# A three-stage kernel in which the gated block's weight items are begun one item ahead and rounds of a gate normalization move to later places

## The chip, the core and the metric

The kernel runs on one core of a Trainium2 chip, in one launch. The time is device microseconds of the whole execution, as the median of several runs; a run with a profile gives a trace beside its time. Every time below comes from the times, the page or the trace of the kernel before.

## What is computed

The reference chains three blocks, each of which feeds the next. The first, attention with a bias from a small network, is not touched and is left out here.

```python
def _moe_ref(x, w1, w2, w3, w_out) -> np.ndarray:          # x (1152, 512), w1..w3 (512, 768)
    h = np.maximum(np.maximum(x @ w1, x @ w2), x @ w3)
    return (h @ w_out).astype(np.float32)

def _moe2_ref(x, w_gate, w1, w2) -> np.ndarray:            # N, D, E, F = 1152, 512, 8, 1024
    ...
    logits = x @ w_gate
    logits = logits - logits.max()
    P = np.exp(logits)
    for _ in range(8):
        P /= P.sum(1, keepdims=True) + 1e-09
        P /= P.sum(0, keepdims=True) + 1e-09
        P *= N / E
    out = np.zeros((N, D), dtype=np.float32)
    for e in range(E):
        h = np.maximum(x @ w1[e], 0.0)
        ye = h @ w2[e]
        out += P[:, e:e + 1] * ye
    return out.astype(np.float32)
```

## The kernel before

Everything is issued by one Python function. It writes each engine's program in the order in which its steps are called, and each engine works through its own program in that order, so a step that waits holds up what stands behind it on its engine. A program of waits between engines is worked out from the tiles that they read and write. T is TensorE, V is VectorE (DVE), A is ScalarE (ACT), G is GpSimd (POOL); DMAs are issued by SyncE (SP). A tile's bufs says how many buffers its name has; a tile waits until the last reader of the buffer that it takes is done.

**Gated block** (second block, from about 211 to 368 us of the span, its output product included). Numbers are split into a high and a low part, and every product is three matmuls: high by high, low by high, high by low. Weights come as 64-bit words in 24 items, in the order of `w_items`: first the three matrices of slice f = 0, then for each of six slices f the three `w` items of the next slice and one `o` item (a part of w_out). One item goes through `prep_w64`: ScalarE takes the absolute value of the upper words into a tile ww (L113), VectorE makes four passes over it (L114, L115, L117, L119, of which the last two read the raw words wr as well), ScalarE copies the high part (L121, wh or woh), and GpSimd subtracts it to get the low part (L122, wl or wol). For an `o` item VectorE also takes a maximum (L111). When an item is through, the DMA of item i + 2 is issued, since there are two raw buffers wr; ww has two buffers as well.

The loop runs over six slices f and three groups g of 384 tokens. A group's matmuls are `m1_mm` (L657): two matrices into m01, 24 matmuls, and the third into p2, 12. Behind the first two ScalarE copies m01 to t1 (L886), VectorE takes the maximum (L888), then, after p2, a second one (L891), and ScalarE writes hh (L892); VectorE's low part and maximum of the group stand in the next one (L895, L799). In between `w_step(6)` and `w_step(4)` issue the next six and four steps of the weight items. Then w_out's product (L1069) gives 16 tiles in the order of `k`; ScalarE evicts them with a scale into acc (L1073), and the steps of `sched[k]` are issued behind tile k.

**Experts** (third block). The program goes up0, up1, up2, down0, up3, up4, down1, up5, up6, down2 and so on to the end: `up(n)` makes half an expert's hidden layer in seven products (L1218) out of 2x2 blocks of x and w1 and sums of them, into the banks x, y and z; ScalarE snaps a bank into s (L1226), VectorE joins a product to it (L1230), ScalarE writes the high part hh (L1234) and VectorE the low part hl (L1239). After each product `then(seg)` issues what `between` and `extra` hold for that place. `x_steps(s)` names the sums of x's blocks for token half s: t1, t2, tb, t4 on VectorE (L971), `h2` to `h6` their high parts (xth, L965, ScalarE) and `l2` to `l6` their low parts (xtl, L961). `m_top` and `m_spread` bring one maximum to all partitions and make the scalars cx, with which the first snapshot is scaled. `down(h)` makes nine output tiles t (L1298), evicted into acc by ScalarE for h = 0 (L1303) and by VectorE else (L1309 for h = 1, L1314); behind tile t it issues the weight work of the coming halves (`todo`: prep_f, L937 to L956, and prep_2, L1029 to L1031).

**The gates' normalization** is eight rounds, each `rows()` (L1147 to L1150) and then `cols(bank)`: one matmul with ones (L1154) and four VectorE instructions (L1155 to L1158), all on the tile P of 128x72. Before, they stand behind tiles of down0, in up3, up4 and down1. P is needed first by `pool_scale`, which multiplies acc by expert 0's gate on GpSimd (L68, nine times), and by `gains(2)` in up6.

## Time and profile before

| what | value |
|---|---|
| median of 3 runs | 1092.28 us (1091.94 to 1093.19) |
| the profiled execution's own time | 1092.72 us |
| its span in the trace | 1090.9 us |
| mean granted TensorE clock | 0.989 |
| TensorE busy | 1051.1 us, 96% of the span |
| VectorE busy | 799.6 us, 73% |
| ScalarE busy | 589.2 us, 54% |
| GpSimd busy | 408.9 us, 37% |

Busy time is the time in which at least one instruction of the engine runs; matmuls follow each other before the one before has ended, so that their durations overlap. A busy share of 96% is a mean over stages: where an engine stops is read from the list of its waits, each with what released it, and what the other engines do in such a stretch from the busy time by stretch and from the groups of instructions by line (busy time, mean duration of one, and the idle time just before them, with what ended it). A timeline gives single instructions with start and duration; "xN" behind a row joins N like ones.

### The profile page before, as it was taken

To read this page: it belongs to the slowest core of one execution; us is meant where nothing else is said; L and a number is where in the kernel's file an instruction comes from. 1 tells how busy PE (TensorE), PEld (TensorE's weight loads), DVE (VectorE), ACT (ScalarE), POOL (GpSimd) and SP (SyncE) were. 2 spreads that over 40 slices of the span, in tenths; PEclk is the share of its full clock that TensorE was granted. 3 is DMA by queue.
4 is the path that set the end of the run, shared out by engine and by line. 5 is a ranking of instruction groups with operands and counts; after the bars stand their busy time and mean duration, and the time that the engine had idled before them with its cause. 6 is when DMAs were issued, how large, how long until landed. Compare 5 with 4: busy or idle time off the path is not lost.

```text
span 1090.9 us, 18480 instructions
## 1 busy us (share of the span) xinstructions
PE 1051.1 (96%) x7163; PEld 736.3 (67%) x7163; DVE 799.6 (73%) x1549; ACT 589.2 (54%) x1003; POOL 408.9 (37%) x285
## 2 busy tenths in 40 slices
PE   7789999999999999999999999999999999999998
PEld 3269988999889765655756657566466575665753
DVE  8989999778776878867677566676776666767633
ACT  7989988434334666444544536445455364454530
POOL 6996998122222424053231312412223124132220
PEclk8989999999999999999999999999999999999999
DMA  5888664233324012120221211302212113020002
GB/s 190 273 242 263 225 192 119 65 108 113 94 58 155 21 42 73 29 63 21 63 63 40 63 35 50 82 20 64 56 46 64 35 50 82 20 44 6 1 1 87
DMA packets 40757, 90.48 MB, mean 83 GB/s; under 512 B 8095, under 2 KB 11102, under 8 KB 39774
## 3 DMA queue, kind: packets, MB, share of 16 engines
q1 hardware_dynamic: 40526, 89.01, 28.6%
q8 instruction: 56, 0.92, 0.4%
q10 hardware_dynamic: 144, 0.29, 0.1%
q14 instruction: 31, 0.25, 0.1%
HBM read 75.20 MB, written 13.30 MB: 81 GB/s over the span
## 4 chain that ended last, share of the span: by engine, by line
PE 65%; DVE 20%; ACT 5%; DMA 4%; issue 4%; POOL 2%; DVEq 0%; ACTq 0%; SPq 0%; POOLq 0%
PE d L1298 27%; PE x L1218 11%; PE y L1218 8%; PE z L1218 7%; PE sc L468 3%; PE o L1069 2%; PE pv L606 2%; PE m L657 2%; PE pt L554 2%; DMA all<-peaks 2%; DVE pk L799 1%; DVE ng L485 1%; DVE ww L114 1%; DVE ww L119 1%; DMA peaks<-pj 1%
## 5 line engine op out<-in xcount | busy, mean ns | idle before, releaser
L1298 PE MATMUL d<-w2h,hh 128*128 128x512 f16 x576 | 218.3, 379 | 1.8 <-DVE acc L1309 1.7
L1298 PE MATMUL d<-w2h,hl 128*128 128x512 f16 x576 | 218.3, 379 | 0.2 <-DVE hl L1239 0.2
L1298 PE MATMUL d<-w2l,hh 128*128 128x512 f16 x576 | 218.3, 379 | 0.0
L1218 PEld LDWEIGHTS <-w1h 128*128 128x128 f16 x1792 | 175.0, 98 | 53.3 <-issue 6.4
L1298 PEld LDWEIGHTS <-hh 128*128 128x128 f16 x1152 | 112.5, 98 | 134.8 <-issue 3.4
L950 POOL TENSOR_TENSOR w1l<-wf,w1h 128x768 f16<-128x768 f32 x32 | 55.7, 1742 | 304.4 <-ACT w1h L949 270.7
L1234 ACT ACTIVATE hh<-s 128x576 f16<-128x576 f32 x128 | 87.3, 683 | 129.0 <-DVE s L1230 101.5
L1239 DVE SCALAR_TENSOR_TENSOR hl<-s,hh 128x576 f16<-128x576 f32 x128 | 112.4, 879 | 48.1 <-ACT hh L1234 45.6
L1314 DVE SCALAR_TENSOR_TENSOR acc<-d,kh,acc 128x512 f32<-128x512 f32 x126 | 94.0, 746 | 67.1 <-PE d L1298 65.6
L1031 POOL TENSOR_TENSOR w2l<-w2r,w2h 128x512 f16<-128x512 f32 x64 | 77.4, 1221 | 120.0 <-ACT w2h L1030 120.0
L1218 PEld LDWEIGHTS <-w1l 128*128 128x128 f16 x896 | 87.7, 98 | 22.7 <-issue 0.6
L1298 PEld LDWEIGHTS <-hl 128*128 128x128 f16 x576 | 56.3, 98 | 68.6 <-DVE hl L1239 0.7
L956 POOL TENSOR_TENSOR w1l<-wf,w1h 128x1024 f16<-128x1024 f32 x32 | 69.2, 2164 | 75.9 <-ACT w1h L953 75.9
L937 ACT ACTIVATE wf<-wr,pw 128x1024 f32<-128x1024 f32 x32 | 36.5, 1141 | 96.9 <-DVE pm L772 96.9
L1226 ACT ACTIVATE s<-x,cx 128x576 f32<-128x576 f32 x96 | 70.4, 733 | 27.0 <-PE x L1218 26.4
L1230 DVE SCALAR_TENSOR_TENSOR s<-z,cx,s 128x576 f32<-128x576 f32 x64 | 52.3, 817 | 42.9 <-ACT s L1226 27.7
L1218 PE MATMUL x<-xth,w1h 128*128 128x288 f16 x384 | 78.5, 286 | 0.7 <-ACT s L1226 0.7
L1218 PE MATMUL x<-xtl,w1h 128*128 128x288 f16 x384 | 78.6, 286 | 0.4 <-DVE xtl L961 0.4
L1218 PE MATMUL x<-xth,w1l 128*128 128x288 f16 x384 | 78.4, 286 | 0.0
L953 ACT ACTIVATE w1h<-wf 128x1024 f16<-128x1024 f32 x32 | 33.6, 1049 | 82.9 <-DVE wf L946 82.9
L657 PE MATMUL m<-xh,wl 128*128 128x384 f32 x216 | 74.1, 343 | 2.9 <-POOL wl L122 2.9
L657 PE MATMUL m<-xh,wh 128*128 128x384 f32 x216 | 73.9, 342 | 2.5 <-DVE t L888 1.4
(227 smaller groups left out, 2371.7 us busy)
## 6 DMA issues: line engine op xcount, KB each, us to landing
wr<-in_moe_w SPq DMA_DIRECT2D x50, 512.0 KB, 3.6
w2r<-in_moe_w SPq DMA_DIRECT2D x64, 256.0 KB, 2.6
bias_f<-bo SPq DMA_DIRECT2D x36, 295.5 KB, 3.6
bias<-bias_f SPq DMA_DIRECT2D x32, 288.0 KB, 2.9
qk<-in_qk SPq DMA_DIRECT2D x7, 1152.0 KB, 7.2
wr<-in_moe_w_out SPq DMA_DIRECT2D x6, 512.0 KB, 3.5
vr<-in_v SPq DMA_DIRECT2D x8, 320.0 KB, 6.9
bias<-bias_f SPq DMA_DIRECT2D x16, 144.0 KB, 4.9
```

Of the source, the lines that this page charges most:

```text
L657: T.matmul(out=p[:, :TG], lhsT=ws[:, 128 * c:128 * c + 128], rhs=xs[:, c, TG * g:TG * g + TG], start=(c == 0 and n == 0), stop=(c == 3 and ...
L937: A.activation(out=t[:, 0:4], in_=w1r.pop(n), func=AF.Identity, scale=w_pow[n // 2, 1][:, 2:3])
L950: G.tensor_tensor(out=lo[:, 0:3], in0=t[:, 1:4], in1=hi[:, 0:3], op=ALU.subtract)
L956: G.tensor_tensor(out=lo[:, 3:7], in0=t[:, 4:8], in1=hi[:, 3:7], op=ALU.subtract)
L1031: G.tensor_tensor(out=lo, in0=r, in1=hi, op=ALU.subtract)
L1218: T.matmul(out=ps[bank][:, s, :SH], lhsT=ws[:, i, c, :], rhs=xs[:, j, c, s * SH:s * SH + SH], start=(start and k == 0), stop=(k == 5), **kw)
L1226: A.activation(out=t, in_=src, func=AF.Identity, scale=c)
L1230: V.scalar_tensor_tensor(out=out, in0=z, scalar=scale, in1=out, op0=ALU.mult, op1=ALU.add)
L1234: A.activation(out=o, in_=src, func=AF.Relu)
L1239: V.scalar_tensor_tensor(out=l, in0=src, scalar=0.0, in1=o, op0=ALU.max, op1=ALU.subtract)
L1298: T.matmul(out=pd, lhsT=hs[:, fh, 128 * t:128 * t + 128], rhs=ws, start=(k == 0), stop=(k == 11))
L1314: V.scalar_tensor_tensor(out=acc[:, t, :], in0=pd, scalar=kh[:, 1 + t:2 + t], in1=acc[:, t, :], op0=ALU.mult, op1=ALU.add)
```

## The change

It has three parts. (1) ScalarE's Abs of weight item i + 1 is issued among the VectorE passes of item i, between the second and the third (`start_w64`); from the start of the gated block on, every third raw item has a third buffer `wr3`, and the load that follows an item is that of item i + 3 in place of i + 2 (`load_item(5)` at the start makes up for the one that is missing). The tiles wh and wl of even slices come from one pool, of odd ones from another, three buffers each. (2) Of `x_steps(1)`, t1 is issued behind tile 14 in place of 15 and h2 is the first high part; tb, h4 and h5 go from behind tile 15 into up0. (3) The fifth row and fourth column round of down0, the pair in up3 and the column round of down1 leave their places; up5 gets two pairs, up6 one column round, up4's second pair stands one product earlier, and `pool_scale` goes from up5 to up6. The number of rounds stays eight.

```diff
@@ -88,8 +88,13 @@
 
-            def load_w64(src):
-                r = w1p.tile([128, 1024], I32, tag="wr", name="wr", bufs=2)
+            third = []
+
+            def load_w64(src, n):
+                if third and n % 3 == 2:
+                    r = third[0].tile([128, 1024], I32, tag="wr3", name="wr", bufs=1)
+                else:
+                    r = w1p.tile([128, 1024], I32, tag="wr", name="wr", bufs=2)
                 dma(r, src.bitcast(I32))
                 return r
 
@@ -98,22 +103,31 @@
-            def prep_w64(r, hi, lo, top_to=None):
-
-                words = r.rearrange("p (a n t) -> p a n t", a=4, t=2)
+            w_abs = {}
+
+            def start_w64(i):
+
+                if i in w_raw and i not in w_abs:
+                    top = w_raw[i].rearrange("p (a n t) -> p a n t", a=4, t=2)[:, :, :, 1]
+                    w_abs[i] = w1p.tile([128, 4, 132], I32, tag="ww", name="ww", bufs=2)
+                    A.activation(out=w_abs[i].bitcast(F32)[:, :, :128], in_=top.bitcast(F32), func=AF.Abs)
+
+            def prep_w64(i, hi, lo, top_to=None):
+
+                start_w64(i)
+                words = w_raw.pop(i).rearrange("p (a n t) -> p a n t", a=4, t=2)
                 top, low = words[:, :, :, 1], words[:, :, :, 0]
-
-                wp = w1p.tile([128, 4, 132], I32, tag="ww", name="ww", bufs=2)
+                wp = w_abs.pop(i)
                 w, f = wp[:, :, :128], wp.bitcast(F32)[:, :, :128]
                 hi, lo = (x.rearrange("p (a n) -> p a n", a=4) for x in (hi, lo))
 
                 peak = [] if top_to is None else [
                     lambda: V.tensor_reduce(out=top_to, in_=f, op=ALU.max, axis=AX.XY, apply_absolute_value=True)]
                 return [
-                    lambda: A.activation(out=f, in_=top.bitcast(F32), func=AF.Abs),
                     lambda: V.tensor_scalar(out=f, in0=f, scalar1=2.0 ** -15, scalar2=None, op0=ALU.max),
                     lambda: V.tensor_scalar(out=w, in0=w, scalar1=3, scalar2=0x3FFFFFFF,
                                             op0=ALU.logical_shift_left, op1=ALU.bitwise_and),
+                    lambda: start_w64(i + 1),
                     lambda: V.scalar_tensor_tensor(out=w, in0=top, scalar=-0x40000000, in1=w,
                                                    op0=ALU.bitwise_and, op1=ALU.bitwise_or),
                     lambda: V.scalar_tensor_tensor(out=w, in0=low, scalar=29, in1=w,
@@ -126,13 +140,13 @@
             w_at, w_steps = [0], []
-            w_pool = [w1p, 3]
+            w_pool = [w1p, None, None]
...
             def load_item(n):
                 if n < len(w_items):
                     kind, i = w_items[n]
                     w_raw[n] = load_w64(a[f"moe_w{i % 3 + 1}"][i // 3] if kind == "w"
-                                        else a["moe_w_out"][128 * i:128 * i + 128])
+                                        else a["moe_w_out"][128 * i:128 * i + 128], n)
@@ -143,10 +157,10 @@
                             return
                         kind, k = w_items[i]
                         if kind == "w":
-                            wt[k] = [w_pool[0].tile([128, 512], F32R, tag=t, name=t, bufs=w_pool[1]) for t in ("wh", "wl")]
-                        w_steps.extend(prep_w64(w_raw.pop(i), *(wt[k] if kind == "w" else wo[k]),
+                            wt[k] = [w_pool[k // 3 % 2].tile([128, 512], F32R, tag=t, name=t, bufs=3) for t in ("wh", "wl")]
+                        w_steps.extend(prep_w64(i, *(wt[k] if kind == "w" else wo[k]),
                                                 top_to=None if kind == "w" else mo[0][:, 18 + k:19 + k]))
-                        w_steps.append(lambda: load_item(i + 2))
+                        w_steps.append(lambda: load_item(i + (3 if third else 2)))
                         w_at[0] += 1
@@ -855,7 +869,9 @@
                 wol = [hp.tile([128, DM], F32R, name=f"wol{f}") for f in range(6)]
                 wo.update({f: (woh[f], wol[f]) for f in range(6)})
                 with pool("mp", bufs=2) as mp:
-                    w_pool[:] = mp, 6, None
+                    w_pool[1] = mp
+                    third.append(mp)
+                    load_item(5)
...
                          8: [b_all] + xs_("t1", "tb", "h2", "l2"), 9: xs_("h3", "h5", "t2") + pf1[1:3], 10: xs_("l3", "l5", "h4") + pf1[3:4],
                          11: xs_("l4", "t4") + pf1[4:6] + [pk(1, 2, 0)], 12: xs_("h6", "g6") + [bs1[0], pk(1, 2, 1), pk(1, 2, 2)],
                          13: [bs1[1], p2(0), pk(1, 2, 3), lambda: peak_join(*SC)], 14: [p2(1), lambda: peak_send(SC[0])],
-                         15: [lambda: last.update(x_steps(1))] + [end(n) for n in ("t1", "t2", "tb", "h3", "h4", "h5", "h2", "l2")]}
+                         15: [end(n) for n in ("t2", "h2", "l2", "h3")]}
+                sched[14] += [lambda: last.update(x_steps(1)), end("t1")]
@@ -1179,7 +1196,8 @@
-                between = {(0, 0): [m_top, end("l3")], (0, 1): [m_spread, end("l4"), end("l5")], (0, 2): [end("t4")],
+                between = {(0, 0): [m_top, end("h4"), end("l3")],
+                           (0, 1): [m_spread, end("l4"), end("tb"), end("h5"), end("l5")], (0, 2): [end("t4")],
                            (0, 3): [end("h6"), end("l6")], (0, 6): [p2(2)], (1, 5): [p2(3)],
@@ -1301,15 +1319,13 @@
                         if h == 0:
 
                             A.activation(out=acc[:, t, :], in_=pd, func=AF.Identity, scale=kh[:, 0:1])
-                            if t in (2, 4, 6, 8):
+                            if t in (2, 4, 6):
                                 cols(ps_u)
-                            if t in (0, 2, 4, 6, 8):
+                            if t in (0, 2, 4, 6):
                                 rows()
                         elif h == 1:
                             V.scalar_tensor_tensor(out=acc[:, t, :], in0=pd, scalar=kh[:, 0:1], in1=acc[:, t, :],
                                                    op0=ALU.mult, op1=ALU.add)
-                            if t == 2:
-                                cols(ps_u)
                         else:
                             V.scalar_tensor_tensor(out=acc[:, t, :], in0=pd, scalar=kh[:, 1 + t:2 + t], in1=acc[:, t, :],
                                                    op0=ALU.mult, op1=ALU.add)
@@ -1323,11 +1339,12 @@
                         extra = {}
                         if n == 1:
                             extra = {i: [f] for i, f in enumerate(prep_f(2))}
-                        for seg in {3: (4,), 4: (1, 5)}.get(n, ()):
+                        for seg in {4: (1, 4), 5: (1, 4)}.get(n, ()):
                             extra.setdefault(seg, []).extend((lambda: cols(ps_d), rows))
-                        if n == 5:
+                        if n == 6:
+                            extra[1] = [lambda: cols(ps_d)]
                             for t in range(NTT):
-                                extra.setdefault(t % 7, []).append(
+                                extra.setdefault(2 + t % 5, []).append(
                                     lambda t=t: pool_scale(acc[:, t, :], acc[:, t, :], P[:, t, 0:1]))
                         if n and (n % 2 == 0 or n == 4 * NE - 1):
                             extra.setdefault(3, []).append(lambda n=n: gains(n // 2 - (n % 2 == 0)))
```

On ScalarE in the gated block (slice f = 1), with the numbers of the tiles: before,

```order
L886 ACTIVATE t1_3862<-m01_3860 128x384
L121 ACTIVATE wh_3853<-ww_3855 128x512
L113 ACTIVATE ww_3899<-wr_3837 128x4x128
L892 ACTIVATE hh_3629<-t2_3863 128x384
L121 ACTIVATE wh_3897<-ww_3899 128x512
L886 ACTIVATE t1_3925<-m01_3923 128x384
```

and at the same place of the changed kernel:

```order
L902 ACTIVATE t1_3866<-m01_3864 128x384
L135 ACTIVATE wh_3857<-ww_3835 128x512
L113 ACTIVATE ww_3905<-wr_3841 128x4x128
L908 ACTIVATE hh_3631<-t2_3867 128x384
L135 ACTIVATE wh_3901<-ww_3861 128x512
L902 ACTIVATE t1_3929<-m01_3927 128x384
```

Before, the Abs that writes ww_3899 is followed by the high part of that same item; now the high part behind the Abs of ww_3905 is that of ww_3861, the item before it.

On ScalarE between the gated block's last tile and the first expert's second snapshot: before,

```order
L1073 ACTIVATE acc_3606<-o_5172,xs_3610 128x288
L965 ACTIVATE xth_4713<-t_5194 128x2x288
L965 ACTIVATE xth_4713<-t_5196 128x2x288
L965 ACTIVATE xth_4713<-t_5195 128x2x288
L965 ACTIVATE xth_4713<-acc_3606 128x2x288
L1226 ACTIVATE s1_5275<-x_5234,cx_5231 128x576
```

and now:

```order
L1090 ACTIVATE acc_3608<-o_5176,xs_3612 128x288
L981 ACTIVATE xth_4713<-acc_3608 128x2x288
L981 ACTIVATE xth_4713<-t_5172 128x2x288
L981 ACTIVATE xth_4713<-t_5174 128x2x288
L981 ACTIVATE xth_4713<-t_5173 128x2x288
L1244 ACTIVATE s1_5275<-x_5231,cx_5228 128x576
```

The copy out of acc (h2) goes from the last to the first place; the copy ahead of s1 is now h5, out of tb (t_5173), and tb stands on VectorE behind the scalars cx and l4:

```order
L1197 TENSOR_SCALAR cx<-cx,xs 128x1
L977 TENSOR_TENSOR xtl<-t,xth 128x2x288
L987 TENSOR_TENSOR t<-acc 128x576
L977 TENSOR_TENSOR xtl<-t,xth 128x2x288
L1248 SCALAR_TENSOR_TENSOR s_5275<-z,cx,s_5275 128x576
```

On VectorE at the start of up5, with the numbers of the tiles: before,

```order
L1230 SCALAR_TENSOR_TENSOR s_6397<-z,cx,s_6397 128x576
L1239 SCALAR_TENSOR_TENSOR hl<-s_6397,hh 128x576
L1230 SCALAR_TENSOR_TENSOR s_6447<-y,cx,s_6447 128x576
L1239 SCALAR_TENSOR_TENSOR hl<-s_6447,hh 128x576
L1270 TENSOR_TENSOR s_6431<-s_6477,s_6431 128x576
```

and now:

```order
L1248 SCALAR_TENSOR_TENSOR s_6371<-z,cx,s_6371 128x576
L1172 TENSOR_REDUCE col<-pc 128x8
L1173 TENSOR_SCALAR col<-col 128x8
L1174 RECIPROCAL col<-col 128x8
L1175 SCALAR_TENSOR_TENSOR P<-P,col 128x72
L1164 TENSOR_REDUCE row<-P 128x9
L1165 TENSOR_SCALAR row<-row 128x9
L1166 RECIPROCAL row<-row 128x9
L1167 TENSOR_TENSOR P<-P,row 128x72
L1257 SCALAR_TENSOR_TENSOR hl<-s_6371,hh 128x576
```

The eight instructions of a pair stand between the first join and its low part; the same eight stand again behind the second join (s_6426).

## Rows read from the trace of the kernel before

**Rows 1.** Waits of TensorE, whole span: waited for, us in total, times, longest us

```profile
PE m L657 <- POOL wl L122: 2.9, 4, 0.8
...
PE y L1218 <- ACT s L1226: 2.4, 2, 2.1
PE d L1298 <- DVE acc L1309: 1.7, 2, 0.9
...
PE m L657 <- DVE t L888: 1.4, 3, 0.6
...
PE m L657 <- ACT wh L121: 1.0, 1, 1.0
PE z L1218 <- DVE col L1155: 0.8, 1, 0.8
```

**Rows 2.** Timeline of TensorE, 229:231: start, duration us, instruction, idle before

```profile
229.05 0.34 PE L657 MATMUL m<-xh,wh 128*128 128x384 f32 x1
229.22 0.34 PE L657 MATMUL m<-xl,wh 128*128 128x384 f32 x1
230.21 0.44 PE L657 MATMUL m<-xh,wl 128*128 128x384 f32 x1 [0.65 <-POOL wl L122]
230.49 0.33 PE L657 MATMUL m<-xh,wh 128*128 128x384 f32 x1
```

**Rows 3.** Busy time by stretch: length, busy of five engines, PEclk, DMA share, GB/s

```profile
229.00:312.00 83.00, 77.64 (x437) 74.95 (x436) 65.44 (x117) 32.00 (x62) 21.85 (x17) 1.00 0.41 107
309.00:313.00 4.00, 2.16 (x11) 1.53 (x10) 2.76 (x6) 1.98 (x4) 1.28 (x1) 0.99 0.40 131
313.00:316.40 3.40, 3.40 (x13) 3.37 (x12) 3.30 (x6) 1.19 (x3) 0.47 (x1) 0.51 0.00 0
481.40:491.70 10.30, 10.30 (x86) 8.23 (x85) 5.78 (x7) 6.88 (x11) 10.30 (x10) 1.00 0.31 92
```

**Rows 4.** VectorE by line, 229:312: busy us, mean ns, idle before and releaser

```profile
L114 DVE TENSOR_SCALAR ww<-ww 128x512 f32<-128x512 f32 x17 | 12.8, 753 | 12.9 <-ACT ww L113 12.9
...
L115 DVE TENSOR_SCALAR ww<-ww 128x512 int32<-128x512 int32 x16 | 6.8, 424 | 0.4
...
L825 DVE TENSOR_REDUCE pj<-pk 128x1 f32<-128x2 f32 x1 | 0.2, 154 | 1.7 <-ACT acc L99 1.7
```

**Rows 5.** GpSimd by line, 229:312

```profile
L122 POOL TENSOR_TENSOR wl<-ww,wh 128x512 fp32r<-128x512 f32 x13 | 16.8, 1291 | 50.1 <-ACT wh L121 38.2 <-issue 11.8
```

**Rows 6.** ScalarE by line, 229:312

```profile
L113 ACT ACTIVATE ww<-wr 128x512 f32<-128x512 f32 x17 | 11.1, 654 | 2.4 <-DMA wr<-in_moe_w 2.4
```

**Rows 7.** Timeline of VectorE, 414.9:417.2 and 433:438

```profile
414.97 0.23 DVE L1155 TENSOR_REDUCE col<-pc 128x8 f32<-128x72 f32 x1 [0.24 <-PE pc L1154]
...
416.67 0.23 DVE L1150 TENSOR_TENSOR P<-P,row 128x72 f32<-128x72 f32 x1
...
433.02 0.22 DVE L1155 TENSOR_REDUCE col<-pc 128x8 f32<-128x72 f32 x1
...
435.62 1.72 DVE L1148 TENSOR_SCALAR row<-row 128x9 f32<-128x9 f32 x1
```

**Rows 8.** Timeline of GpSimd, 433:438

```profile
435.19 2.12 POOL L956 TENSOR_TENSOR w1l<-wf,w1h 128x1024 f16<-128x1024 f32 x1
```

**Rows 9.** Timeline of VectorE, 368.8:377

```profile
371.51 0.75 DVE L971 TENSOR_TENSOR t<-acc 128x576 f32<-128x576 f32 x1
...
373.85 0.21 DVE L1180 TENSOR_SCALAR cx<-cx,xs 128x1 f32<-128x1 f32 x1
```

**Rows 10.** Timeline of ScalarE, 368.8:377

```profile
373.84 0.74 ACT L1226 ACTIVATE s<-x,cx 128x576 f32<-128x576 f32 x1 [0.29 <-DVE cx L1178]
```

**Rows 11.** Timeline of TensorE, 372:379

```profile
375.57 0.28 PE L1218 MATMUL x<-xtl,w1h 128*128 128x288 f16 x1 [0.41 <-DVE xtl L961]
...
376.67 0.41 PE L1218 MATMUL y<-xth,w1h 128*128 128x288 f16 x2
```

**Rows 12.** GpSimd by line, 480:500

```profile
L68 POOL TENSOR_SCALAR acc<-acc,P 128x512 f32<-128x512 f32 x9 | 8.7, 986 | 0.0
```

## Prediction

> **What bounds the kernel now.** TensorE is busy for 96% of the span in the first part of the page, so only what makes it stop can be won. I read its waits first [rows 1]; there the reader is to see that three of them belong to the gated block's L657 (2.9, 1.4 and 1.0 us in 4, 3 and 1 times) and three to the start of the experts (2.4, 1.7 and 0.8 us), all of it work that this diff touches. Then I read TensorE's own starts at one such wait [rows 2]: matmuls follow each other by 0.17 us, the one that waited starts 0.65 us late, and the next comes 0.28 after it, 0.44 instead of 0.34 long; start to start the stall costs 230.49 - 229.22 - 2 x 0.17 = 0.93 us, that is its idle time and 0.28 more. Then the busy time in stretches [rows 3], to see which engine fills the stretch behind a wait, and the groups of VectorE, GpSimd and ScalarE in the gated block's 83 us [rows 4 to 6], to see what the busy time consists of and what each engine was waiting for.
>
> **Gated block, weight items one ahead.** In the stretch of 83.00 us TensorE is busy for 77.64, so idle for 5.4; the three waits give 2.9 + 1.4 + 1.0 = 5.3 [rows 1, 3]. With 0.28 us for each of the eight stalls that is 5.3 + 2.2 = 7.5 us. Right behind the stretch's end its granted clock is 0.51 for 3.40 us in which 13 matmuls run [rows 3], after 4.00 us in which TensorE was busy for only 2.16: at 0.17 us each they would take 2.2, so the low clock costs 1.2. That is 8.7 us to be had.
>
> What is late is VectorE. It is busy for 65.44 us of 83.00, and it idles 12.9 us ahead of the first pass over a weight item, L114, always for ScalarE's Abs of that item [rows 4]: 0.76 us for each of 17 items, near the 0.654 us that one Abs takes [rows 6]. The Abs stands on ScalarE just ahead of its own item's hi, and its VectorE passes follow at once. The change puts it a whole item earlier, so this idle time goes. The same Abs also waits 2.4 us for a weight load [rows 6]; with a third raw buffer a load is issued one item sooner, 83/17 = 4.9 us, and this wait goes too.
>
> A cover may go with it. L114 takes 753 ns where L115, the same form and size, takes 424 [rows 4]: L114 runs beside the previous item's lo on GpSimd (L122, 1291 ns [rows 5]). In the normalization the same is plain: a scalar step on 128x9 took 1.72 us and ended at 437.34, just behind a GpSimd operation that ended at 437.31, where a multiplication on 128x72 alone takes 0.23 [rows 7, 8]. So a VectorE step of this form started while GpSimd runs stands still until that ends. When L114 no longer waits for the Abs, it comes sooner after the previous hi and stands still for longer. Bounds: nothing more than now (0.33 an item) and a whole lo (1.29). Without blocking VectorE needs 65.4 - 17 x 0.33 = 59.8 us, and 1.7 for the size pass that it waits for [rows 4]; TensorE needs 83.0 - 7.5 = 75.5. The room is (75.5 - 61.5)/17 = 0.82 an item. I take 0.6, since L122 begins only behind the hi pass on ScalarE, in which VectorE can do a step of the group first. That leaves TensorE the bound, but not in every group: I leave 1.5 us of the 8.7 where single groups stay late. Term: **-7.2 us**, between -3.0 (blocking at 1.1) and -8.7.
>
> The Trainium skill, page "SBUF — State Buffer", section "Who interferes with whom", says that VectorE and GpSimd share one port pair under an exclusive lock, that a VectorE instruction with two SBUF inputs or in a two-port mode blocks fully beside a GpSimd one that reads SBUF, and that issue order decides which. The trace agrees in the blocked step's 1.72 us. Taken alone, that rule would let L114 be held for a whole lo each time, and the sum would be about -2.8; that is rival A.
>
> **Normalization, fewer rounds in down0, two more in up5.** One C and R pair (a column and a row round, eight VectorE instructions from L1155 to L1150) takes from 414.97 to 416.90 alone, 1.93 us; beside GpSimd its first six instructions take from 433.02 to 437.34, 4.3 us, and so the pair some 4.8 [rows 7]. The second one stands in up3, where z waits 0.8 us for col and y waits up to 2.1 us for a snapshot [rows 1]; the change takes it out. The 0.8 goes; of the snapshot's 2.4 I take the 2.1 that lies there: **-2.8** (bounds 0 if the weight items' ScalarE work alone keeps the snapshot late, -3.2 if both go). In down1 TensorE waits 1.7 us in two times for the eviction [rows 1], behind a column round that the change removes: four of eight instructions, half of 1.93 = 0.97 us. It clears the first (0.9) and half of the second: **-1.3** (bounds 0 and -1.7).
>
> The two pairs that are added to up5 stand ahead of hl, and z's bank is free only after the joins behind them. In the stretch of up5 VectorE is busy for 5.78 of 10.30 us [rows 3], so 4.5 us of slack. Two pairs cost 3.86, and one of them meets the lo of a weight part on GpSimd (2.12 us [rows 8]), a block of at most 1.72: 5.6, which is 1.1 over. With two column matmuls more on TensorE, 0.17 each: **+1.5** (bounds 0, if the block falls elsewhere, and 5.5, if both pairs take 4.8 like the one at 433: 9.7 - 4.5 + 0.3). The one column round that goes to up6 is half a pair, 0.97, below that slack. The nine scalings of acc on GpSimd [rows 12] go from up5 to up6: 8.7 us of a stretch of 10.30, covered by up6's own products, since the first use of acc is the first eviction behind them; without that cover each would cost 0.99. What they block on VectorE in up5 now, they block in up6. Sum of this part: **-2.6**, between -4.9 and +5.5.
>
> **Start of the first expert.** Before, ScalarE does all four xth copies (h2 to h5) and then the first product's snapshot s1; VectorE does t1, t2 and tb (L971) ahead of the scalars that s1 needs. Now t1 goes one tile of the gated block's output earlier, and tb, its copy h5 and l4 come between the scalars and s1, because h5 stands ahead of s1 on ScalarE. The scalars end at 374.06 now and s1 at 374.58 [rows 9, 10]. Two steps of L971 leave from ahead of the scalars, 0.75 us each [rows 9]: they end at 372.6, or up to 0.7 later if l3 has to wait for its copy. Behind them l4 and tb take 0.75 each, h5 and s1 0.74 each [rows 9, 10]: s1 ends at 375.6 to 376.3. The second product into s1's bank starts then. Now it starts earlier but stands before its fourth matmul until 375.57, for l4; the nine left take until 376.67 [rows 11], so twelve take 1.47, and the product behind starts at 377.1 to 377.8 in place of 376.67. Term: **+0.8**, between +0.4 and +1.2.
>
> **Sum.** -7.2 - 2.6 + 0.8 = -9.0 us. The profiled execution took 1092.72 us around its span of 1090.9; it becomes 1083.7. The median of the three runs shown is 0.44 lower, so 1083.3.
>
> **The rivals.**
> Forecast as above, 0.50. Low bound: all of the gated gain, the normalization's -4.9 and +0.4 at the first expert give -13.2; since all three together are unlikely I end the range a little above that, at 1079.5.
>
> Low clock again: if TensorE idles about as much at the first expert as in the 4.00 us before the low stretch (2.16 busy), the clock may fall there as it did at 313, for 1.2 us more; 1084.7. Against it: the idle time there comes in pieces. 0.17.
>
> Rival A, the lock takes the gated gain: each L114 is held 1.0 to 1.29 us, VectorE needs 61.5 + 17 x 1.29 = 83.4 us, all of the present stretch. For it: L114 comes nearer to the lo. Against: there is group work between. Only the 2.6 and the 0.8 and 1 us of clock remain, -2.8: about 1089.5. 0.12.
>
> Rival B, the added pairs run beside GpSimd in up5 as the one at 433 did, 4 us more: 1087.3. For it: GpSimd is busy for all of 10.30 us there [rows 3]. Against: most of that is the scaling, which leaves. 0.10.
>
> Rival C, slower: the Abs now stands ahead of hi and of the evictions of m on ScalarE, and needs one of two ww buffers, free only when GpSimd's lo of the item before the present one is done. If that lo is late, Abs waits and the evictions (t, hh) wait behind it, and VectorE behind those. It decides where the wait is over the 0.76 us an item that goes; at 1.0 us an item it costs 17 x 0.24 = 4.1, and the 7.2 are not won: with the other parts 1094.6. Against it: GpSimd idles 38.2 us for ScalarE's hi [rows 5], so the lo is seldom late. 0.06.
>
> Rival D: the gains at L657 turn up as waits at the block's last product, and nothing changes: 1092.3. 0.05.
>
> **How the numbers follow.** The forecast, the low clock, rival B and most of the ground toward A lie between 1079.5 and 1089.0, where I end the range: A's upper half, C and D, some 0.17, lie outside, and a little below. A measurement of this kernel can tell about 0.2%, 2.2 us, from no change. Faster by more than that: forecast, low clock, A and B, 0.89, less 0.01 for A's upper end, 0.88; the same, D and A's end, 0.06; slower, C, 0.06.
>
> **What would show it.** In the gated block: the waits of m for wl, t and wh below 1.5 us together, VectorE's idle time ahead of L114 (now two lines on in the code, same form) below 3 us and its mean up to 0.9 or 1.1; no stretch at a clock of 0.51 at the end. In up3: no wait of z for col, and that of y below 0.5. In down1: one wait for acc at most. In up5 to up6: a wait of about 1 us of z for s. At the first expert: s1 near 376, and y's snapshot behind it. Wrong would be: L114's mean at 1.2 or over (A), ScalarE idle ahead of Abs for POOL (C), C and R pairs of 4 us in up5 (B), or a gated block that is shorter by over 9 us.

## The result, and the profile after

The change takes 1082.68 us in the median of five runs (1080.69 to 1084.42), before 1092.28 (1091.94 to 1093.19): the ratio is 0.9911, with a 95% interval of 0.9899 to 0.9924, so 8.3 to 11 us faster. The forecast was 1083.3. The profiled execution of the change is the fastest of its five, 1080.69 us around a span of 1078.9, so that the two traces lie 12.0 us apart where the medians lie 9.6.

The waits of TensorE after, those that answer to [rows 1]:

```profile
PE x L1236 <- ACT s L1244: 3.4, 3, 2.3
...
PE y L1236 <- ACT s L1244: 0.9, 2, 0.6
PE z L1236 <- DVE s L1248: 0.6, 1, 0.6
...
PE d L1316 <- DVE acc L1327: 0.4, 1, 0.4
...
PE pc L1171 <- DVE P L1167: 0.3, 1, 0.3
```

No line for m is left in this list: the 5.3 us at L657 are gone, and so is z's wait for col. Of the waits behind attention one has grown by over 0.5 us: x for s, from 0.7 to 3.4, 2.3 of them in one piece. The busy time of the gated block's stretch, which answers to the first of [rows 3], and below it the groups of VectorE, ScalarE and GpSimd there, as in [rows 4 to 6]:

```profile
229.00:306.00 77.00, 77.00 (x445) 77.00 (x445) 73.03 (x126) 34.35 (x64) 22.67 (x17) 1.00 0.39 104
```
```profile
L131 DVE SCALAR_TENSOR_TENSOR ww<-wr,ww 128x512 int32<-128x512 int32 x18 | 15.9, 885 | 0.4
L133 DVE SCALAR_TENSOR_TENSOR ww<-wr,ww 128x512 int32<-128x512 int32 x18 | 12.4, 691 | 0.5
L127 DVE TENSOR_SCALAR ww<-ww 128x512 f32<-128x512 f32 x17 | 10.7, 631 | 0.2 <-ACT ww L113 0.2
L128 DVE TENSOR_SCALAR ww<-ww 128x512 int32<-128x512 int32 x17 | 9.4, 554 | 0.4
```
```profile
L113 ACT ACTIVATE ww<-wr 128x512 f32<-128x512 f32 x16 | 10.8, 674 | 17.3 <-POOL wl L136 11.1 <-DMA wr<-in_moe_w_out 3.2 <-POOL wol L136 2.1
```
```profile
L136 POOL TENSOR_TENSOR wl<-ww,wh 128x512 fp32r<-128x512 f32 x12 | 15.9, 1325 | 38.9 <-ACT wh L135 23.7 <-issue 11.0 <-PE m L671 4.3
```

TensorE is busy for all of 77.00 us, and VectorE for 73.03 of them, where it had been busy for 65.44 of 83.00. The reader is to see what became of VectorE's 12.9 us of idle time ahead of the first pass: 0.2 us are left. The waiting moved to ScalarE, whose Abs now waits 11.1 + 2.1 us for GpSimd's low parts and 3.2 for loads; it costs nothing here, since VectorE is an item behind. The stretching of the passes by GpSimd is there too, but spread: L127, L128 and L131 take 631, 554 and 885 ns, while L115 of before took 424 on the same size [rows 4] and L133 here, a pass of the form of L131, takes 691; so the three are 0.21 + 0.13 + 0.19 = 0.53 us an item longer.

Four starts of TensorE mark the stages of a trace: the first L657 (m) behind attention, the transposition pmw behind the gated block, pmx at the first expert, and the first product of down0. Before and after:

```profile
210.84 0.34 PE L657 MATMUL m<-xh,wh 128*128 128x384 f32 x1
...
330.43 0.27 PE L1000 MATMUL pmw<-ident,mho 128*2 128x128 f32 x1 [0.26 <-DVE mho L987]
...
369.70 0.27 PE L1170 MATMUL pmx<-ident,m 128*1 128x128 f32 x1 [0.36 <-DVE m L1083]
...
406.81 0.39 PE L1298 MATMUL d<-w2h,hh 128*128 128x512 f16 x1
```
```profile
210.10 0.34 PE L671 MATMUL m<-xh,wh 128*128 128x384 f32 x1
...
320.58 0.27 PE L1016 MATMUL pmw<-ident,mho 128*2 128x128 f32 x1 [0.26 <-DVE mho L1003]
...
359.86 0.27 PE L1187 MATMUL pmx<-ident,m 128*1 128x128 f32 x1 [0.36 <-ACT xth L981]
...
397.43 0.39 PE L1316 MATMUL d<-w2h,hh 128*128 128x512 f16 x1
```

These marks and those of the other traces, with the first product of down3 as the last one (545.94 before, 533.98 after), give this table (us; c1 and c2 are the change again, on two other chips; the experiments follow):

| trace | gated block, m to pmw | first expert, pmx to down0 | down0 to down3 |
|---|---|---|---|
| before | 119.59 | 37.11 | 139.13 |
| after; c1; c2 | 110.49; 110.49; 110.49 | 37.57; 38.13; 38.97 | 136.55; 137.79; 137.86 |
| e1, gated part alone | 110.49 | 37.08 | 141.17 |
| e2, first expert alone | 117.86 | 37.56 | 139.81 |
| e3, rounds alone | 120.23 | 37.11 | 137.71 |
| e4; e11, h5 late | 110.49; 110.94 | 36.11; 36.09 | 137.94; 137.54 |
| e5, third buffer without Abs ahead | 117.05 | 38.43 | 137.47 |
| e6, Abs ahead with two buffers | 120.80 | 40.20 | 137.58 |
| e8, pair in up6 | 110.49 | 38.14 | 136.96 |
| e9, low part on VectorE | 118.62 | 37.58 | 137.85 |
| e10, h5 late and pair in up6 | 110.93 | 36.11 | 137.10 |

Whole runs hold more than these stages. In the nine traces whose order of work is that of the change up to the first mark (after, c1, c2, e1, e4, e6, e8, e10, e11), that mark comes at 208.5 to 212.6 us. So a difference of 1 or 2 us between whole runs can't be given to a stage without the marks.

### The profile page after: what moved, and what is told of

Read it like the earlier page. It is cut to its first block, busy times and chain, and to the rows that moved or that the text cites. A ratio compares the mean times of both kernels' runs of the same rounds, so it can differ in the third digit from the quotient of the medians.

```text
span 1078.9 us, 18481 instructions
## 1 busy us (share of the span) xinstructions
PE 1044.3 (97%) x7163; PEld 734.6 (68%) x7163; DVE 800.3 (74%) x1549; ACT 590.3 (55%) x1003; POOL 410.0 (38%) x285
## 4 chain that ended last, share of the span: by engine, by line
PE 74%; DVE 14%; ACT 5%; DMA 3%; issue 2%; POOL 2%; DVEq 0%; ACTq 0%; POOLq 0%
PE d L1316 27%; PE x L1236 11%; PE m L671 11%; PE y L1236 8%; PE z L1236 7%; PE sc L482 3%; PE o L1086 2%; PE pv L620 2%; PE pt L568 2%; DMA all<-peaks 2%; DVE pk L813 2%; DVE ng L499 1%; DVE s L1248 1%; POOL s L356 1%; DVE hl L1257 1%
## 5 line engine op out<-in xcount | busy, mean ns | idle before, releaser
L671 PE MATMUL m<-xh,wh 128*128 128x384 f32 x216 | 72.9, 337 | 0.0
L671 PE MATMUL m<-xh,wl 128*128 128x384 f32 x216 | 72.8, 337 | 0.0
```

The costliest lines, as they stand in the source:

```text
L671: T.matmul(out=p[:, :TG], lhsT=ws[:, 128 * c:128 * c + 128], rhs=xs[:, c, TG * g:TG * g + TG], start=(c == 0 and n == 0), stop=(c == 3 and ...
```

## The experiments

The kernel before took 1096.3 us in the median on the three chips of the experiments (15 to 17 runs each, 1093.8 to 1099.7), 4 us more than on the first; so each kernel is compared with the runs of its own chip. Where an expectation names a whole time, it is worked out from the first chip's; the difference is what can be held against it.

**The three parts alone (e1, e2, e3).** Each is before with one part of the change's diff.

> Only the first part: Abs one item ahead, third raw buffer, the two pools of wh and wl. Theory (VectorE stood idle for the Abs, and the stalls of L657 with the low clock behind them were all of it): -7.2 to -8.7 us, so 1083.6 to 1085.1; no wait of m on wl, t or wh in the trace, idle time ahead of L114's counterpart below 1 us, and no stretch at clock 0.51 near 313. Rival 1 (the lock gives it back): mean of that step at 1.2 us or more and less than 3 us won. Rival 2 (the gain of the whole change comes from the rounds and the first expert): less than 2 us won.

> Only the second part: t1 one tile earlier, h2 first, tb, h4 and h5 between the scalars and the first snapshot. Theory (h5 ahead of s1 on ScalarE delays the second product into x more than the earlier scalars give): +0.4 to +0.8 us, 1092.7 to 1093.1, with one wait of x for s of about 2.3 us at the first expert and the 1.1 us wait of pmx gone. Rival (the edit helps, since the scalars come 1.2 us earlier): -0.5 to -1.2 us, 1091.1 to 1091.8, with less idle time of TensorE there.

> Only the third part: the rounds and the scaling of acc. Theory (each part as forecast: -2.8 in up3, -1.3 in down1, +1.5 in up5): -2.6 us, 1089.7, with the waits of y for s at 440 and of z for col at 433 gone, one wait for acc left in down1, and one of about 0.7 us of z for s behind up5. Rival 1 (the weight items' copies keep the snapshot late without the pair as well): y still waits 1 to 2 us for s in up3, -1 us at most, 1091.3. Rival 2 (up5's pairs run beside GpSimd): +1 us or more in all.

The gated part alone: 1088.20 us, ratio 0.9915 (0.9899 to 0.9932). Its gated block takes 110.49 us, to the hundredth what the change takes, with no wait at L657; the old block takes 117.86 and 120.23 on the same chip (e2, e3). It is the bulk of the change, and TensorE is the bound there. VectorE still idles 1.6 us ahead of the first pass, where less than 1 was expected. Both rivals fall.

The first expert alone: 1095.34 us, 0.9993 (0.9982 to 1.0004), not to be told from no change. The stage is 0.45 us longer (37.56 for 37.11), and its waits are those expected:

```profile
PE x L1220 <- ACT s L1228: 2.9, 2, 2.3
```

The rounds alone: 1092.38 us, 0.9961 (0.9947 to 0.9975). From down0 to down3 it takes 137.71 us, where the old places take 139.81 on the same chip (e2), and 141.17 with a stretch of low clock (e1); so 2.1 of the 4.0 us in the medians are shown in this stage. The waits of z for col and the long one of y went, but two of 0.5 and 0.6 us came in up3, so that rival 1 holds for a part:

```profile
PE x L1218 <- ACT s L1226: 1.2, 3, 0.5
...
PE y L1218 <- ACT s L1226: 0.9, 2, 0.6
...
PE z L1218 <- DVE s L1230: 0.7, 1, 0.7
```

In whole runs the three parts give -8.1, -1.0 and -4.0 us, together -13.1, more than the change's -10.7 and -9.6 (c1, c2). By stages they give what the change gives: 110.49, 37.56 and 137.71 beside 110.49, 38.13 and 38.97 (with the low clock), and 137.79 and 137.86. That the excess lies outside these stages is likely, but not shown: e3's trace reaches the first mark 2.6 us ahead of e2's, with the same order of work.

**The buffer without Abs ahead (e5), and Abs ahead without the buffer (e6), beside the change (c1).** Both keep the other two parts of the change.

```diff
 e5:
-                    lambda: start_w64(i + 1),
...
+                    lambda: A.activation(out=f, in_=top.bitcast(F32), func=AF.Abs), 
 e6:
-                    third.append(mp)
-                    load_item(5)
```

> The change itself, unaltered, on the chip and beside the runs of before that the next three share, so that they can be set against it. Theory: -8 to -11 us against before, with no wait of m on wl, t or wh; the chance part of it is TensorE's clock, which is 0.5 for 3.4 us at differing places.

> The change with the Abs of each weight item back at the item's own start; the third raw buffer and the earlier loads stay. Theory (VectorE's idle time ahead of L114 is for the Abs itself, the load is the small part): VectorE still idles 9 to 12 us there in the same stretch, six to eight waits at L657 stay, and the kernel is 5.5 to 8 us slower than the change. Rival (the late load was the cause): within 2 us of the change.

> The change with two raw buffers as before, the Abs still one item ahead. Theory: ScalarE now waits for the load in order, ahead of the copies of m and of hi, 1 to 1.5 us an item; 1 to 4 us slower than the change, with waits of m for t or wl back in part. Rival (the load comes in time all the same, for an item takes 4.9 us and a load 3.6): within 0.5 us of the change.

The change: 1085.62 us, 0.9898 (0.9878 to 0.9918). The buffer alone: 1091.71, 0.9956 (0.9941 to 0.9971), 6 us slower than the change. In its trace VectorE's idle time ahead of the first pass is 10.4 us (229 to 312), seven waits at L657 stay, and ScalarE waits for no load:

```profile
L127 DVE TENSOR_SCALAR ww<-ww 128x512 f32<-128x512 f32 x17 | 13.2, 775 | 10.4 <-ACT ww L126 10.4
```
```profile
L126 ACT ACTIVATE ww<-wr 128x512 f32<-128x512 f32 x17 | 11.1, 652 | 0.0
```

So the Abs ahead takes the main part of the 12.9 us, as the theory has it. What the buffer takes alone is 1.1 to 2.6 us: with the old order that idle time is 12.9 us (before), 13.0 (e3) and 11.5 (e2), and ScalarE's wait for a load, one of 2.4 or 2.5 us, is in the first two of these traces and not in e2's.

The Abs ahead with two buffers: 1095.76, 0.9995 (0.9983 to 1.0006). All of the gated gain is gone: the kernel is 10.1 us slower than the change, where the theory had 1 to 4; this was the surprise. The gated block takes 120.80 us, 3.8 more than without the Abs ahead (e5). ScalarE's Abs and VectorE's low part of a group in 229 to 312 of this trace:

```profile
L113 ACT ACTIVATE ww<-wr 128x512 f32<-128x512 f32 x17 | 11.5, 674 | 38.7 <-DMA wr<-in_moe_w 26.8 <-DMA wr<-in_moe_w_out 9.8 <-POOL wl L136 2.2
```
```profile
L909 DVE TENSOR_TENSOR hl<-t,hh 128x384 fp32r<-128x384 f32 x12 | 6.6, 552 | 6.8 <-ACT hh L906 6.8
...
L902 DVE TENSOR_TENSOR t<-m,t 128x384 f32<-128x384 f32 x11 | 6.1, 552 | 2.9 <-ACT t L900 2.9
```
```profile
302.89 0.66 ACT L113 ACTIVATE ww<-wr 128x512 f32<-128x512 f32 x1 [6.61 <-DMA wr<-in_moe_w]
303.45 0.51 ACT L906 ACTIVATE hh<-t 128x384 fp32r<-128x384 f32 x1
303.87 0.62 ACT L135 ACTIVATE wh<-ww 128x512 fp32r<-128x512 f32 x1
304.39 0.47 ACT L900 ACTIVATE t<-m 128x384 f32<-128x384 f32 x1
```

VectorE does not wait for the Abs here either; it waits 6.8 us for hh and 2.9 for t. In the timeline the Abs stands still for 6.61 us for its load, and hh, hi and t, which had nothing to do with that load, come out one behind the other after it; TensorE then waits 2.9 us for t, and from 306.2 its clock is 0.51 for 3.5 us. That is rival C's mechanism with a load in place of GpSimd's low part. This load took 7.1 us from issue to landing, where the median of such loads in the trace is 3.7, so that one stall makes up 2.9 of the 6.2 us that TensorE waits at L671 (m for t, wl and wh). Most of the others are waits of 0.7 to 0.8 us for wl and wh like those of before; how much of them the loads cause is not shown.

**h5 behind the snapshots (e4, e11), beside the change (c2).**

```diff
-                           (0, 1): [m_spread, end("l4"), end("tb"), end("h5"), end("l5")], (0, 2): [end("t4")],
+                           (0, 1): [m_spread, end("l4"), end("tb")], (0, 2): [end("h5"), end("l5"), end("t4")],
```

> The whole change, but h5 and l5 stand behind the snapshots of the first and second product instead of ahead of s1 (tb stays). Theory (s1 stands behind tb and h5, in order, and that is the 2.3 us wait of x): s1 follows the scalars at once, x waits 0.2 to 0.5 us, and the kernel is 1.5 to 2.1 us faster than the change, 1080.6 to 1081.2. Rival (the second product waits for l4 or the third for l5 instead, as late): within 0.5 us of the change, 1082.2 to 1083.2.

> The change itself once more, beside the next three, as what they are set against. Theory: -8 to -11 us against before; where TensorE's clock falls to 0.5 at the first expert, it does so behind the wait of x for s of 2.3 us.

> The change with h5 and l5 behind the snapshots, as in e4, now beside the change on one chip. Theory: 1.4 us less idle time at the first expert, as the two traces already show, and no fall of the clock there, which in the change comes in some executions and costs 1 us more: 1.5 to 3 us faster than the change, and its runs closer together. Rival (the clock falls at another place instead): 0 to 1 us faster, and runs as far apart as the change's.

In the change ScalarE (first fence) and TensorE (second) show the chain that the forecast worked out:

```profile
364.46 0.68 ACT L981 ACTIVATE xth<-t 128x576 f16<-128x576 f32 x1 [3.37 <-DVE t L987]
365.05 0.72 ACT L1244 ACTIVATE s<-x,cx 128x576 f32<-128x576 f32 x1
```
```profile
365.82 0.41 PE L1236 MATMUL x<-xth,w1h 128*128 128x288 f16 x2 [2.34 <-ACT s L1244]
```

In e4 the snapshot comes at once, and the same product starts 2.3 us sooner (pmx is at 359.86 in the change and at 359.87 here):

```profile
362.77 0.74 ACT L1244 ACTIVATE s<-x,cx 128x576 f32<-128x576 f32 x1 [1.67 <-DVE cx L1195]
363.53 0.74 ACT L1244 ACTIVATE s<-y,cx 128x576 f32<-128x576 f32 x1
364.47 0.68 ACT L981 ACTIVATE xth<-t 128x576 f16<-128x576 f32 x1 [0.20 <-DVE t L987]
```
```profile
363.56 0.41 PE L1236 MATMUL x<-xth,w1h 128*128 128x288 f16 x2
```

The stage takes 36.1 us, 1.5 less than in the change's trace without low clock and 1.0 less than before; a later product into x waits 0.8 us for its snapshot instead of 0.5. e4 took 1082.68 us, 0.9871 (0.9856 to 0.9886), on a chip on which the change was not run; e11, on the chip of c2, 1083.92, 0.9883 (0.9867 to 0.9899), where the change took 1086.79, 0.9900 (0.9883 to 0.9918): 2.9 us in the medians, while the intervals against before overlap. The four runs of e11 lie within 1.1 us, the six of c2 within 4.2; both are as the theory had it, with few runs. In the two traces the stage is 2.9 us shorter: 1.5 by the chain (37.57 to 36.09) and 1.4 by the clock at this place (38.97 to 37.57). TensorE before the product of c2 starts and behind it, in c2 and at the same times in e11:

```profile
362.80:367.40 4.60, 2.27 (x18) 1.56 (x16) 3.75 (x11) 1.35 (x3) 1.93 (x2) 1.00 0.40 108
367.50:370.80 3.30, 3.30 (x15) 2.07 (x15) 1.42 (x3) 0.82 (x2) 0.00 (x0) 0.50 0.06 5
```
```profile
362.80:367.40 4.60, 4.53 (x37) 3.38 (x35) 4.47 (x13) 2.17 (x3) 1.82 (x2) 1.00 0.44 108
367.50:370.80 3.30, 3.10 (x25) 2.22 (x23) 2.53 (x4) 1.89 (x3) 0.00 (x0) 1.00 0.01 0
```

In c2 TensorE is busy for 2.27 of 4.60 us and then granted 0.50 of its full clock; in e11 it is busy for 4.53 and keeps its clock. Of the eight traces with the change's order here (after, c1, c2, e2, e5, e6, e8, e9), five show the low clock between 367 and 382 us, none of the six others (before, e1, e3, e4, e10, e11). The three without it take 37.56 to 37.58 us for the stage, the five with it 38.13 to 40.20.

**The second pair in up6 (e8), and with h5 late (e10).**

```diff
-                        for seg in {4: (1, 4), 5: (1, 4)}.get(n, ()):
+                        for seg in {4: (1, 4), 5: (1,), 6: (1,)}.get(n, ()):
...
-                            extra[1] = [lambda: cols(ps_d)]
+                            extra[3] = [lambda: cols(ps_d)]
...
-                                extra.setdefault(2 + t % 5, []).append(
+                                extra.setdefault(3 + t % 4, []).append(
```

> The change with up5's second pair of rounds moved to up6, the last column round two products later, and the scaling of acc one product later. Theory (up5's two pairs overfill VectorE by about 1 us): the waits of pc for P and of z for s behind up5 (0.3 and 0.65 us) go and nothing comes in up6; 1.0 to 1.5 us faster than the change. Rival (up6 is as full, or the scaling now comes late for the first eviction of down2): waits of z for s or d for acc of 0.5 us or more in up6 to down2, and no gain.

> h5 and l5 late and also up5's second pair of rounds in up6. Theory: the two gains add, 2 to 4 us faster than the change, 0.5 to 1 faster than h5 late alone. Rival (the later rounds only move the wait to down2): the same as h5 late alone.

The change's up5, VectorE, GpSimd and TensorE:

```profile
471.89 0.22 DVE L1172 TENSOR_REDUCE col<-pc 128x8 f32<-128x72 f32 x1
472.15 1.79 DVE L1173 TENSOR_SCALAR col<-col 128x8 f32<-128x8 f32 x1
```
```profile
471.78 2.13 POOL L972 TENSOR_TENSOR w1l<-wf,w1h 128x1024 f16<-128x1024 f32 x1
```
```profile
475.49 0.44 PE L1171 MATMUL pc<-P,ones 128*128 128x72 f32 x2 [0.30 <-DVE P L1167]
...
480.99 0.41 PE L1236 MATMUL z<-xth,w1h 128*128 128x288 f16 x2 [0.65 <-DVE s L1248]
```

The first scalar step of the pair is held until GpSimd's low part ends (471.78 + 2.13 = 473.91; 472.15 + 1.79 = 473.94), pc and then z are late. With the second pair in up6 both waits are gone from the list, and the stage from down0 to down3 takes 136.96 and 137.10 us, 0.8 less than the change on the same chip each (c1, c2); e10's is 0.4 less than e11's. In whole runs that is too little to tell: e8 1084.63 us beside c1's 1085.62. e10 took 1083.40, 0.9877 (0.9861 to 0.9893); its four runs, 1083.21 to 1083.53, lie below all six of c2's and all four of e11's, so it is the fastest of its chip, by 0.5 us over e11.

**The low part on VectorE (e9).**

```diff
-                    lambda: G.tensor_tensor(out=lo, in0=f, in1=raw(hi), op=ALU.subtract)] + peak
+                    lambda: V.tensor_tensor(out=lo, in0=f, in1=raw(hi), op=ALU.subtract)] + peak
```

> The change with the low part of the gated block's weight items on VectorE instead of GpSimd. Theory (VectorE's passes are stretched by GpSimd's lo alone): in the stretch 229 to 306 the passes take 0.42, 0.42, 0.69, 0.69 us in place of 0.63, 0.55, 0.89, 0.69; VectorE's busy time rises only by what is left of the low part (0.2 us an item, 3 us), TensorE stays the bound there, and the time is within 1 us of the change. Rival (the passes are stretched by something else, weight loads or ScalarE's writes): the means stay at 0.55 and above, VectorE has no room left, and waits at L657 come back, 3 us or more slower.

```profile
L131 DVE SCALAR_TENSOR_TENSOR ww<-wr,ww 128x512 int32<-128x512 int32 x16 | 11.0, 687 | 0.3
L133 DVE SCALAR_TENSOR_TENSOR ww<-wr,ww 128x512 int32<-128x512 int32 x15 | 10.3, 690 | 0.4
L136 DVE TENSOR_TENSOR wl<-ww,wh 128x512 fp32r<-128x512 f32 x11 | 7.6, 689 | 6.0 <-ACT wh L135 6.0
L128 DVE TENSOR_SCALAR ww<-ww 128x512 int32<-128x512 int32 x16 | 6.8, 425 | 0.4
...
L127 DVE TENSOR_SCALAR ww<-ww 128x512 f32<-128x512 f32 x15 | 6.3, 418 | 0.0
```

The means are those expected, 418, 425, 687 and 690 ns: it was GpSimd's low part that stretched the passes. The expected time was not: 1098.17 us, 1.0012 (0.9999 to 1.0026), 11 us over c2; in the traces, 7.4 us apart, the gated block is 8.1 us longer. VectorE is not full (65.2 of 77.0 us busy); it now stands for 6.0 us (and 2.7 more ahead of wol) until ScalarE has written hi, in the middle of its program, and m waits for t again (3.6 us in six times). The time came out as the rival had it, by another mechanism. What I had summed was busy time, without the new wait in order.

## Why the prediction was right, term by term

**Gated block, -7.2 taken, -9.1 measured** between the two profiles (119.59 to 110.49); e2 and e3, with the old block, take 117.86 and 120.23, so -7.4 to -9.7. The mechanism is shown: the Abs ahead takes VectorE's idle time away (after and e1 against e5), and TensorE has no stall left there. The term's lower bound was -8.7, and the forecast named a gated block shorter by over 9 us as a sign of being wrong; between these two profiles it is just that, and on the chip of e1 to e3 it is so beside one old block of two. The blocking that I took at 0.6 us an item is 0.53, spread over three passes and not on L114 alone, which even became shorter (631 ns for 753, where I had expected 0.9 or more). Two steps of the working failed. The 1.5 us that I left for late groups were not lost: all waits went. And the low clock at 313 was counted as a fixed 1.2 us of the old block, while e2 and e3 show stalls of the same kind without it; it comes in some executions. Of the 2.4 us between e2 and e3, a part is the wait of m for wh, 1.2 us in e3 and none in e2; ScalarE waits 2.5 us for a late load in e3 and for none in e2. Rival A is out by the 631 ns, rival D by the 39.27 us from pmw to pmx, the same before and after.

**The third buffer** I priced at a wait of 2.4 us that goes. That wait is one late load, which not every execution has (e2), and a wait for loads is still there (3.2 us now). The buffer is worth far more: without it the Abs ahead gives nothing (e6). Rival C is no rival of this change, though its place was right: ScalarE does wait 13.2 us for low parts, but ahead of work that is not yet due. ScalarE idle ahead of the Abs for POOL was named as a sign of C; it came without harm, so it was no sign.

**Rounds, -2.6 taken.** By the lists of waits, z for col (0.8), y for s (2.4), d for acc (1.7) and z for s (0.5) became y 0.9, x at up3 about 0.5 of its 3.4, d 0.4 and 0.2, z 0.6, pc 0.3: 5.4 to 2.9, or -2.5. up3 gave a little less than the 2.8, for the copies of the weight items still hold its snapshots; down1 what was forecast (1.7 to 0.4; 0.5 to 1.1 on the other chips); up5's overshoot is there with its block of 1.79 us beside GpSimd, 0.95 us of waits where I took 1.1. Rival B is out: one block, not several. What the term lacks is a wait late in down2 for an eviction, 0.4 to 0.8 us, which ten of the eleven traces with the new places have (not the profile after), and none of the three with the old.

**First expert, +0.8 taken (0.4 to 1.2), +0.46 measured** in the profiles with full clock. The chain is the one worked out: s1 ends 365.77 - 359.86 = 5.9 us behind pmx, and 375.6 - 369.70 = 5.9 was my lower end. But the low clock that I gave only 0.17 as a rival, because the idle time would come in pieces, came in five of eight traces: the waits had become one of 2.3 us. Between the two profiles the stages give -9.1 - 2.6 + 0.5 = -11.2; of the other 0.8 us of the 12.0, 0.7 lie ahead of the first mark (210.84 and 210.10). With 0.6 to 1.4 us for the clock that is -9.8 to -10.6, near the -9.6 of the medians. So the sum of -9.0 came near partly by luck: the gated term was 1.9 us too small, and the clock at the first expert was left out. That the spread of the change's runs is the clock's is not shown, since one run of each kernel has a trace. On the first chip the two runs with a mean granted clock of 0.994 took 1080.69 and 1080.95 us, the three with 0.989 to 0.992 took 1082.68 to 1084.42; but the slowest of c2's, 1087.81, had 0.994.

Three small sums of the working are off: 0.8 + 2.1 in up3 is 2.9 and not 2.8; the low-clock rival is 1083.3 + 1.2 = 1084.5 and not 1084.7; and with L114 held for 1.1 us an item VectorE needs 61.5 + 17 x 1.1 = 80.2 of the 83.0 us, so that the bound is -2.8 and not -3.0. None moves the forecast by more than 0.1 us.

## What to carry to other kernels

An operation put ahead on an engine that works in order must have its input there as early, or it holds up all that stands behind it: the load has to be moved ahead by as much as the operation, with the buffer that this needs, and the two are one edit. A sum of busy time shows whether an engine has room, not whether its order lets it use it; for each moved step ask what it now waits for, and who stands behind it. And several small waits joined to one long one can cost more than their sum: at the first expert the low clock came behind the joined wait in five of eight traces, and in none of the three with the old pieces. At 313 us of before it came behind short waits too, so these runs give it as a chance and not as a rule.

## What the runs showed of the hardware

At the first expert the granted clock fell to 0.50 of full speed behind a stretch in which TensorE was busy for 2.27 of 4.60 us (c2), and did not behind the like stretch of the profile after (2.28 of 4.60), so that the same order gives both. It cost the stage 0.6 to 1.4 us for a low stretch of 3.4 us, and 2.6 for one of 6.8 (e6). In e1 it fell at 432 us behind the wait of 2.1 us in up3, which the rounds' new places remove; behind the same wait of 2.1 us in the profile before it did not. A scalar step of VectorE on 128x8 took 1.79 us beside GpSimd and 0.17 alone, and a pass over 128x512 with two inputs was stretched from 0.69 to 0.89 in the mean; with the low part of the gated block moved off GpSimd (e9) that stretching of the pass went. The Trainium skill, page "SBUF — State Buffer", section "Who interferes with whom", describes a lock on a port pair shared by VectorE and GpSimd, under which the engine that comes second stands still until the other's instruction ends. The step of 1.79 us agrees: it ended at 473.94 us, GpSimd's at 473.91.
